# A linear-attention and mixture-of-experts kernel: tile loads widened to 128 rows, its start and early iterations reordered

## The chip, the cores and the metric

The kernel runs on one core of one Trainium2 chip, as one launch. The metric is device microseconds of that core, lower is better. The engines are TensorE (PE; its weight loads are shown as PEld), VectorE (DVE), ScalarE (ACT), GpSimd (POOL) and SyncE (SP), which issues most of the DMAs.

## The reference, cut to what matters

Three stages follow each other: a linear attention with a decay (4 batches, 8 heads, 768 positions, head size 48), an expert layer that sends each of the 3072 tokens to one of 8 experts, and a dense block with three gates. The change touches the first.

```python
for t in range(S):                       # 768 positions
    cur = einsum('bhd,bhe->bhde', u[None] * kt, vt)
    y[:, :, t] = einsum('bhd,bhde->bhe', rt, state + cur)
    state = wt[:, :, :, None] * state + einsum('bhd,bhe->bhde', kt, vt)
...
logits = x @ w_gate + modality_bias[modality_id]     # expert by argmax
out[mask] = gate_w[mask, None] * (max(x[mask] @ w1[e], 0) @ w2[e])
...
h = max(max(x @ w1, x @ w2), x @ w3);  return h @ w_out
```

Here rt, kt, vt and wt are the rows of r, k, v and w at position t.

## The kernel before, in words

The attention works on 24 tiles of 128 positions (6 per batch). A tile's r, k and w come transposed: 96 rows (a pair of heads of 48 channels each), and in the free dimension 3 x 4 head pairs x 128 positions. `load_t` brings them into one of four buffers `tq0` to `tq3`, in the 96 partitions from PAD = 16 on, so that each head lies in one half of the 128 partitions. The 16 partitions on both sides must hold harmless values: before the first tile, `pads` and some single fills write 0 for r and k and 1 for w to them (L768, L781 to L788, L798), and nothing overwrites them later. A second load, `load_n` (L816), brings the same tile with positions in partitions (`nat`: v, r and k).

For a tile, `flags` (L843, L845) checks the range of w with two ACT activations, `cut_w` (L854, L855) saves the last decay column of each head pair as `wl` and sets it to 0 in the buffer (times `keep`, which is 1 in the pad rows), so that one long scan over four head pairs starts afresh at each. `scan_f` (L861 to L865) takes the running product of the decays on DVE into the PSUM bank `prod`, `mul_r` (L870) multiplies r by it, `scan_r` (L875, L877) makes the reverse product, and `mul_k` (L882) multiplies k by that. PE then has `ktrans` (L904, copied by ACT as `kn`, L906), `scores` (L891, copied by ACT, L894, and masked by POOL, L895, as `am`), `kv` (L913, the tile's state contribution), `output` (L925, L931) and, behind DVE's `output_x` (L952, the output x), `columns` (L959, copied by ACT, L962) and `logits_of` (L239). `state_a` and `state_b` (L938, L943, L946) carry the state. The term with u goes over POOL (`uterm_a` L828 and L829, `uterm_b` L838) and a DVE sum (`usum` L834).

The order of the work is the order in which the code is written; every engine works its own instructions in that order and waits by semaphores. In iteration i of the main loop (L1017) DVE scans tile i + 2, PE transposes and scores tile i + 1 and makes the output of tile i; loads are issued some tiles ahead, and a load into a buffer waits until the tile that had it is done with it. `warm(n)` puts n filler matmuls on PE (L985); their numbers are in `WARM`. `rows()` (L174 to L221) prepares constants for the routing, in pieces that `slot()` puts into the iterations. From iteration 9 on, `route_between` routes tiles already done, and from iteration 13 on the first expert's weights are loaded. Behind the loop follow the last tiles, the rest of the routing, the experts and the dense block, which the change leaves as they are.

Of the kernel before, what the change touches and what calls it, by code (L numbers as in the profile page):

```python
# [23 lines left out]
P_LO = 1e-22  # L24
BIG = 1000000.0
# [18 lines left out]
WARM = (32, 20, 4, 0, 3, 0)  # L44
# [3 lines left out]
def kernel(ctx: ExitStack, tc: tile.TileContext, rkw_t, v_t, vrk, u, modality, w_gate, bias, w1, w2, v1, v2,  # L48
# [93 lines left out]
    flag = ct([128, NTILE, 2], F32, "flag")  # L142
# [587 lines left out]
    def attention(hooks):  # L730
        with ExitStack() as es:
# [35 lines left out]
            keep = e1.tile([128, 1], F32, name="keep")  # L767
            DVE.memset(tq[0][96:128, 1024:1536], 1.0)  # L768
            DVE.memset(wide, 0.0)
# [14 lines left out]
            def zeros(out, _):  # L784
                for q in range(2):
                    ACT.copy(out[:, q * 512:(q + 1) * 512], wide)
            POOL.memset(tq[0][96:128, 0:1024], 0.0)
            DVE.memset(tq[0][0:PAD, 1024:1536], 1.0)  # L788
            POOL.memset(neglo[:, 0:1], W_LO)
            POOL.memset(neglo[:, 1:2], -W_HI)  # L790
            POOL.memset(keep, 0.0)
            POOL.memset(keep[0:PAD], 1.0)
            POOL.memset(keep[96:128], 1.0)
            POOL.memset(keep[96:PAD + 2 * D], 0.0)
            DVE.memset(d1f, P_LO)
            DVE.memset(v4(d1f)[:, :, 0:1], 1.0)
            DVE.memset(d1r, 0.0)
            POOL.memset(tq[0][0:PAD, 0:1024], 0.0)  # L798
            pads(1, zeros)
            pads(2, DVE.memset, DVE.memset)  # L800
# [3 lines left out]
            pads(3)  # L804
# [35 lines left out]
            def flags(i):  # L840
                wr = tq[i % NB][:, 1024:1536]
                jk = a1.tile([128, 512], BF16, tag="jk", name="jk")
                ACT.activation(out=jk, in_=wr, func=ACTF.Relu, scale=-1.0, bias=neglo[:, 0:1],  # L843
                               accum_out=flag[:, i, 0:1])
                ACT.activation(out=jk, in_=wr, func=ACTF.Relu, scale=1.0, bias=neglo[:, 1:2],  # L845
                               accum_out=flag[:, i, 1:2])

            def cut_w(i):


                last = w_of(i)[:, :, 127:128]
                s = T[i]
                s["wl"] = a2.tile([128, HP, 1], F32, tag="wl", name="wl")
                ACT.copy(s["wl"], last)  # L854
                ACT.activation(out=last, in_=last, func=ACTF.Copy, scale=keep)  # L855

            def scan_f(i):

                s = T[i]
                f = tq[i % NB]  # L860
                DVE.tensor_tensor_scan(out=prod, data0=f[:, 1023:1535], data1=d1f, initial=0.0, op0=ALU.mult, op1=ALU.max)  # L861
# [3 lines left out]
                DVE.tensor_tensor(out=s["pt"], in0=end, in1=s["wl"], op=ALU.mult)  # L865
# [124 lines left out]
            load_t(0, [slice(q, q + 1) for q in (2, 0, 1)])  # L990
# [4 lines left out]
            load_n(1)  # L995
            loads()
            SP.dma_start(out=wg, in_=w_gate.rearrange("(k p) e -> p k e", p=128))
            load_n(2)
            warm(WARM[0])
            flags(0)  # L1000
            for i in range(2):
                cut_w(i)
                scan_f(i)
                mul_r(i)
                scan_r(i)
                mul_k(i)
                if i == 0:
                    flags(1)
                    ktrans(0)
                    scores(0)  # L1010
                    warm(WARM[1])
                uterm_a(i)
            load_t(3)
            load_t(4)
            flags(2)
            cut_w(2)
            for i in range(NTILE - 2):  # L1017
                n = i + 2
# [9 lines left out]
                if i:  # L1028
# [5 lines left out]
                uterm_a(n)  # L1034
# [13 lines left out]
                state_b(i)  # L1048
                slot()
                slot()  # L1050
                for j in (0, 1) if i == 0 else (i + 1,):
                    usum(j)
                    uterm_b(j)
# [10 lines left out]
                if i == 0:  # L1064
# [677 lines left out]
```

## Time and profile before

| | |
|---|---|
| median of 3 runs | 725.69 us (724.01 to 728.71) |
| profiled execution, its own time | 731.36 us |
| its span, from the first to the last instruction | 729.7 us |
| mean granted TensorE clock | 0.978 |
| busy share: PE, DVE, ACT, POOL | 96%, 63%, 45%, 45% |

The profile is of one execution; its span is what the timeline covers, and its own time has the launch around it. A busy engine is one that has an instruction under way; matmuls overlap, so a busy PE is not PE at its peak. Shares over the whole span are averages over stages with different limits.

### The profile page before, as it was taken

What the parts mean: (1) busy time and instruction counts of PE and PEld (TensorE: products, weight loads), DVE (VectorE), ACT (ScalarE), POOL (GpSimd) and SP (SyncE); (2) the same over time, 40 slices, a digit from 0 to 9 for tenths busy, and PEclk for the clock granted to TensorE, in tenths of its full rate; (3) what the DMA queues carried; (4) which work ended last, traced back from release to release, by engine and by line L of the source; (5) the groups of instructions that cost most, each with busy time, mean ns of one, the idle gap of its engine ahead of it and who ended that gap; (6) DMA issues with size and microseconds to landing.
All of it is one profiled execution on the core that took longest, in us unless ns stands there. A gap on an engine that the chain in (4) does not pass through costs nothing.

```text
span 729.7 us, 13002 instructions
## 1 busy us (share of the span) xinstructions
PE 697.3 (96%) x4891; PEld 629.5 (86%) x4892; DVE 456.2 (63%) x848; ACT 331.2 (45%) x720; POOL 326.1 (45%) x385
## 2 busy tenths in 40 slices
PE   8899999998799999999999999999999999999996
PEld 3788879787699999999999888988988989889886
DVE  6888988788395878998989758624234243142230
ACT  5576758764123576766667644321212212112111
POOL 5666667698736677768765424310200201101002
PEclk9899999999789999999999999999999999999998
DMA  8777769991023232232352633010200200000001
GB/s 248 219 225 214 232 171 208 251 284 47 12 67 90 86 109 66 87 87 67 121 196 66 226 108 108 19 69 0 82 6 0 88 1 11 33 1 33 11 1 48
DMA packets 29851, 72.98 MB, mean 100 GB/s; under 512 B 5109, under 2 KB 16149, under 8 KB 29780
## 3 DMA queue, kind: packets, MB, share of 16 engines
q1 hardware_dynamic: 25076, 62.58, 29.6%
q0 software_dynamic: 4704, 9.49, 4.1%
q8 instruction: 40, 0.66, 0.4%
q14 instruction: 31, 0.25, 0.1%
HBM read 83.04 MB, written 14.38 MB: 134 GB/s over the span
## 4 chain that ended last, share of the span: by engine, by line
issue 35%; PE 19%; POOL 5%; DVE 4%; ACT 2%; DMA 2%; POOLq 0%; DVEq 0%; ACTq 0%; SPq 0%
PE mm L1286 6%; PE mm L1287 6%; PE mm L1285 6%; POOL out_dram L1431 3%; DMA w2r<-in_moe_w_dram 2%; ACT w2h L636 1%; DVE w2l L638 1%; DVE t L689 1%; DVE hl L1299 1%; POOL vl L692 1%; DVE ya L678 1%; DVE ya L669 1%; PE tp L1274 0%; ACT hh L1298 0%; DVE ya L665 0%
## 5 line engine op out<-in xcount | busy, mean ns | idle before, releaser
L1411 DVE TENSOR_TENSOR w2r<-mm,w2r 128x512 f32<-128x512 f32 x72 | 49.7, 690 | 138.1 <-PE mm L1287 138.0
L1431 POOL DMA_INDIRECT out_dram<-w2r,oi_all x24 | 26.0, 1082 | 237.5 <-ACT w2r L1430 237.2
L1287 PE MATMUL mm<-w1h,vl 128*128 128x512 f32 x324 | 126.2, 389 | 0.0
L1286 PE MATMUL mm<-w1l,vh 128*128 128x512 f32 x324 | 126.2, 389 | 0.0
L1285 PE MATMUL mm<-w1h,vh 128*128 128x512 f32 x324 | 126.1, 389 | 0.0
L1286 PE MATMUL mm<-hl,w2h 128*128 128x256 f32 x288 | 83.1, 289 | 2.9 <-DVE hl L1299 2.8
L1285 PE MATMUL mm<-hh,w2h 128*128 128x256 f32 x288 | 83.8, 291 | 0.9 <-issue 0.9
L1287 PE MATMUL mm<-hh,w2l 128*128 128x256 f32 x288 | 82.5, 287 | 1.5 <-issue 1.5
L1413 ACT CAST w2h<-w2r 128x512 fp32r<-128x512 f32 x36 | 22.4, 621 | 129.6 <-DVE w2r L1411 129.6
L1285 PE MATMUL mm<-xh,w1h 128*128 128x256 f32 x282 | 81.0, 287 | 0.0
L1286 PE MATMUL mm<-xl,w1h 128*128 128x256 f32 x282 | 80.7, 286 | 0.3 <-issue 0.3
L1287 PE MATMUL mm<-xh,w1l 128*128 128x256 f32 x282 | 80.6, 286 | 0.0
L1287 PEld LDWEIGHTS mm<-w1h,vl 128*128 128x128 f32 x324 | 60.8, 188 | 12.7
L1286 PEld LDWEIGHTS mm<-w1l,vh 128*128 128x128 f32 x324 | 60.8, 188 | 12.5
L1285 PEld LDWEIGHTS mm<-w1h,vh 128*128 128x128 f32 x324 | 60.8, 188 | 12.4
L638 POOL TENSOR_TENSOR w2l<-w2r,w2h 128x384 fp32r<-128x384 f32 x44 | 50.1, 1143 | 33.1 <-ACT w2h L636 32.6
L1286 PEld LDWEIGHTS mm<-hl,w2h 128*128 128x128 f32 x288 | 56.4, 196 | 3.8 <-DVE hl L1299 3.8
L1285 PEld LDWEIGHTS mm<-hh,w2h 128*128 128x128 f32 x288 | 56.3, 196 | 2.9 <-issue 2.9
L1287 PEld LDWEIGHTS mm<-hh,w2l 128*128 128x128 f32 x288 | 56.3, 195 | 0.6 <-issue 0.6
L1286 PEld LDWEIGHTS mm<-xl,w1h 128*128 128x128 f32 x282 | 55.0, 195 | 0.5 <-issue 0.5
L1285 PEld LDWEIGHTS mm<-xh,w1h 128*128 128x128 f32 x282 | 55.0, 195 | 0.1
L1287 PEld LDWEIGHTS mm<-xh,w1l 128*128 128x128 f32 x282 | 54.9, 195 | 0.0
(338 smaller groups left out, 1647.1 us busy)
## 6 DMA issues: line engine op xcount, KB each, us to landing
w1r<-in_moe_w_dram SPq DMA_DIRECT2D x10, 1536.0 KB
w2r<-in_moe_w_dram SPq DMA_DIRECT2D x10, 1536.0 KB
nat<-in_vrk_dram SPq DMA_DIRECT2D x24, 608.0 KB
tq<-in_rkw_t_dram SPq DMA_DIRECT2D x23, 576.0 KB
stg<-in_moe_w_dram SPq DMA_DIRECT2D x18, 384.0 KB
x2t<-raw SPq DMA_DIRECT2D x12, 384.0 KB
w1r<-x2t SPq DMA_DIRECT2D x12, 384.0 KB
xs<-x SPq DMA_DIRECT2D x23, 192.0 KB
```

The costliest lines, as they stand in the source:

```text
L636: ACT.copy(hi, src)
L638: eng.tensor_tensor(out=lo, in0=src, in1=hi.bitcast(F32), op=ALU.subtract)
L669: DVE.tensor_scalar(out=yi, in0=yi, scalar1=3, scalar2=0x3FFFFFFF, op0=ALU.logical_shift_left, op1=ALU.bitwise_and)
L678: DVE.tensor_scalar(out=s["ya"].bitcast(I32), in0=s["t1"], scalar1=-0x800000, scalar2=None, op0=ALU.bitwise_and)
L689: DVE.tensor_tensor(out=tf, in0=tf, in1=hi.bitcast(F32), op=ALU.subtract)
L692: POOL.tensor_tensor(out=lo, in0=s["lf"], in1=s["t1"].bitcast(F32), op=ALU.add)
L1285: PE.matmul(oc, lhsT=wh[:, kk, sl], rhs=xh[:, kk, :], start=first and kk == 0, stop=False)
L1286: PE.matmul(oc, lhsT=wh[:, kk, sl], rhs=xl[:, kk, :], start=False, stop=False)
L1287: PE.matmul(oc, lhsT=wl[:, kk, sl], rhs=xh[:, kk, :], start=False, stop=last and kk == nk - 1)
L1411: DVE.tensor_tensor(out=hv, in0=o, in1=hv, op=ALU.max)
L1413: ACT.copy(self.h2h[:, c, :], hv)
L1431: ins = POOL.indirect_dma_start(out=out[:, :], out_offset=bass.IndirectOffsetOnAxis(ap=ids[q][:, 0:1], axis=0), in_=ob, in_offset=None, bo ...
```

## The change

A tile's load now covers all 128 partitions: since the 96-row blocks of all tiles follow each other in HBM, 16 rows of the block before and 16 of the block behind come along. For the first tile the rows before are missing (its load has 112 rows, and the fills for its first 16 partitions stay), for the last those behind (112 rows, and one fill of its last decay columns). No other buffer is filled beforehand. The foreign rows hold real numbers, so `mul_r` multiplies r also by `mine`, 1 in the tile's own 96 partitions and 0 elsewhere; the last column is set to 0 in all partitions; the product `pt` gets a lower bound, WL_LO. `flags` now comes after `cut_w`, and after `mul_k`, so it checks the 127 other columns; the last columns of all tiles are kept in `wlast` and checked once by `flags_last`. At the start r and k of tile 0 are loaded by ACT's queue and w by SP's, tile 1 is cut before the scores of tile 0, and loads, sums, outputs and filler matmuls of the first two iterations stand elsewhere; `rows()` begins after iteration 2 and no longer after iteration 0.

```diff
-WARM = (32, 20, 4, 0, 3, 0)
+WARM = (26, 9, 4, 0, 3, 0)
...
-            def pads(j, rk=POOL.memset, w=POOL.memset):
-                rk(tq[j][:, 0:1024], 0.0)
-                w(tq[j][:, 1024:1536], 1.0)
...
-            def load_t(i, parts=(slice(0, 3),)):
-                b, c = divmod(i, NC)
+            def load_t(i, parts=(slice(0, 3),), eng=SP):
+                lo = PAD if i == 0 else 0
+                hi = PAD + 2 * D if i == NTILE - 1 else 128
+                if i == NTILE - 1:
+                    POOL.memset(w_of(i)[:, :, 127:128], 1.0)
+                first = 2 * D * i - PAD
                 for q in parts:
-                    SP.dma_start(out=tq[i % NB][PAD:PAD + 2 * D, q.start * 512:q.stop * 512],
-                                 in_=rkw_t[b, c, :, :, q].rearrange("o d q a t -> (o d) (q a t)"))
+                    eng.dma_start(out=tq[i % NB][lo:hi, q.start * 512:q.stop * 512],
+                                  in_=all_t[first + lo:first + hi, q, :].rearrange("r q x -> r (q x)"))
...
-                ACT.activation(out=last, in_=last, func=ACTF.Copy, scale=keep)
+                ACT.activation(out=last, in_=last, func=ACTF.Copy, scale=0.0)
...
-                DVE.tensor_tensor(out=s["rt"], in0=r_of(i), in1=v4(prod), op=ALU.mult)
+                DVE.scalar_tensor_tensor(out=s["rt"], in0=r_of(i), scalar=mine, in1=v4(prod), op0=ALU.mult, op1=ALU.mult)
...
-            load_t(0, [slice(q, q + 1) for q in (2, 0, 1)])
+            load_t(0, [slice(0, 2)], ACT)
+            load_t(0, [slice(2, 3)])
             load_t(1)
             load_n(0)
             load_u()
             load_t(2)
             load_n(1)
+            load_t(3)
+            load_n(2)
             loads()
             SP.dma_start(out=wg, in_=w_gate.rearrange("(k p) e -> p k e", p=128))
-            load_n(2)
+            load_n(3)
             warm(WARM[0])
-            flags(0)
             for i in range(2):
                 cut_w(i)
                 scan_f(i)
+                flags(i)
                 mul_r(i)
                 scan_r(i)
                 mul_k(i)
-                if i == 0:
-                    flags(1)
-                    ktrans(0)
-                    scores(0)
-                    warm(WARM[1])
-                uterm_a(i)
-            load_t(3)
+            ktrans(0)
+            scores(0)
+            uterm_a(0)
+            warm(WARM[1])
+            cut_w(2)
             load_t(4)
-            flags(2)
-            cut_w(2)
             for i in range(NTILE - 2):
                 n = i + 2
-                if i + 5 < NTILE:
-                    load_t(i + 5)
                 kv(i)
...
+                if i == 1:
+                    output_x(0)
                 scan_f(n)
...
+                if i < 2:
+                    usum(i)
+                    uterm_b(i)
+                if i == 0:
+                    uterm_a(1)
+                if i == 1:
+                    warm(WARM[2])
...
-                if i + 3 < NTILE:
+                if 0 < i and i + 3 < NTILE:
                     load_n(i + 3)
+                if i + 5 < NTILE:
+                    load_t(i + 5)
                 output(i)
                 if i + 3 < NTILE:
-                    flags(i + 3)
                     cut_w(i + 3)
...
                 state_b(i)
+                flags(n)
+                if n == NTILE - 1:
+                    flags_last()
...
-                if i == 0:
+                if i == 2:
                     later.append(rows())
```

How this moves instructions on ACT at the start of the program, with the semaphores that each waits for (DMAHW are landings of loads), before; the tile buffers tq0 to tq3 are `tq_160` to `tq_163` here:

```order
L786 ACT_TABLE_LOAD
L786 CAST tq_161<-wide 128x512 [waits DVE_49]
L843 ACTIVATE jk,flag<-tq_160,neglo 128x512 [waits DMAHW0_49,DVE_49,Pool_49]
L845 ACTIVATE jk,flag<-tq_160,neglo 128x512 [waits Activation_49,Pool_49]
L854 COPY wl<-tq_160 128x4
L855 ACTIVATE tq_160<-tq_160,keep 128x4 [waits Activation_49,Pool_49]
L843 ACTIVATE jk,flag<-tq_161,neglo 128x512 [waits DMAHW3_49,Pool_49]
L845 ACTIVATE jk,flag<-tq_161,neglo 128x512 [waits Activation_49]
L906 COPY kn<-tp 128x512 [waits PE_49]
L894 COPY am<-mm 128x512 [waits PE_49] x2
L854 COPY wl<-tq_161 128x4
L855 ACTIVATE tq_161<-tq_161,keep 128x4 [waits Activation_49]
```

And now on the same engine and place; the buffers are `tq_161` to `tq_164`:

```order
L809 DMA tq_161<-in_rkw_t_dram 112x1024 [waits Pool_49]
L858 ACT_TABLE_LOAD [waits DMAHW0_49]
L858 COPY wlast<-tq_161 128x4 [waits DVE_49]
L859 ACTIVATE tq_161<-tq_161 128x4 [waits Activation_49]
L843 ACTIVATE jk,flag<-tq_161,neglo 128x4x127 [waits Pool_49]
L843 ACTIVATE jk,flag<-tq_161,neglo 128x4x127 [waits Activation_49,Pool_49]
L858 COPY wlast<-tq_162 128x4 [waits DMAHW1_49]
L859 ACTIVATE tq_162<-tq_162 128x4 [waits Activation_49]
L843 ACTIVATE jk,flag<-tq_162,neglo 128x4x127
L843 ACTIVATE jk,flag<-tq_162,neglo 128x4x127 [waits Activation_49]
L912 COPY kn<-tp 128x512 [waits PE_49]
L900 COPY am<-mm 128x512 [waits PE_49] x2
```

The cuts of tiles 0 and 1 (COPY wl or wlast and the ACTIVATE behind it) stand ahead of the checks and of tile 0's kn and am copies, and the table load stands behind the wait for the first decay load.

In a usual iteration, again on ACT, the rows before from the state copies of one iteration to those of the next:

```order
L946 COPY sbd_151<-stt_153 64x4x48 x2
L906 COPY kn<-tp 128x512
L894 COPY am<-mm 128x512 x2
L962 COPY xT<-tp 128x384
L843 ACTIVATE jk,flag<-tq_161,neglo 128x512
L845 ACTIVATE jk,flag<-tq_161,neglo 128x512
L854 COPY wl<-tq_161 128x4
L855 ACTIVATE tq_161<-tq_161,keep 128x4
```

And now:

```order
L952 COPY sbd_152<-stt_154 64x4x48 x2
L843 ACTIVATE jk,flag<-tq_162,neglo 128x4x127 x2
L912 COPY kn<-tp 128x512
L900 COPY am<-mm 128x512 x2
L968 COPY xT<-tp 128x384
L858 COPY wlast<-tq_164 128x4
L859 ACTIVATE tq_164<-tq_164 128x4
```

The cut follows the column copy xT directly; the two checks, of a tile whose k is already multiplied, stand between the state copies and the kn copy.

## Rows read from the trace of the kernel before

**Rows 1.** The page's busy time, share of the span and instructions of each engine.
```profile
PE 697.3 (96%) x4891; PEld 629.5 (86%) x4892; DVE 456.2 (63%) x848; ACT 331.2 (45%) x720; POOL 326.1 (45%) x385
```

**Rows 2.** Waits, 0 to 165 us: who waited for whom, us, times, longest.
```profile
DVE prod L861 <- ACT tq L855: 17.1, 14, 3.5
...
POOL nat L828 <- DMA nat<-in_vrk_dram: 7.1, 4, 4.1
DVE sh L834 <- POOL nat L829: 5.4, 5, 1.6
PE tp L959 <- DVE x L952: 5.2, 10, 1.6
```

**Rows 3.** Timeline, 0 to 41 us: start, duration, instruction [idle before <- ended by].
```profile
0.84 1.28 ACT L786 ACT_TABLE_LOAD   x1 [0.70 <-PEq L1727]
...
1.52 2.72 SPq L811 DMA_DIRECT2D tq<-in_rkw_t_dram  x4
...
4.27 0.72 ACT L843 ACTIVATE jk<-tq,neglo 128x512 bf16<-128x512 f32 x1 [1.00 <-DMA tq<-in_rkw_t_dram]
...
5.90 0.18 ACT L854 COPY wl<-tq 128x4 f32<-128x4 f32 x1
...
6.57 1.23 DVE L861 TENSOR_TENSOR_SCAN prod<-tq,d1f 128x512 f32<-128x512 f32 x1 [1.23 <-ACT tq L855]
...
8.72 0.72 ACT L843 ACTIVATE jk<-tq,neglo 128x512 bf16<-128x512 f32 x1 [2.24 <-DMA tq<-in_rkw_t_dram]
...
14.35 1.23 DVE L861 TENSOR_TENSOR_SCAN prod<-tq,d1f 128x512 f32<-128x512 f32 x1 [3.49 <-ACT tq L855]
...
18.73 1.23 DVE L861 TENSOR_TENSOR_SCAN prod<-tq,d1f 128x512 f32<-128x512 f32 x1
...
24.20 1.22 DVE L861 TENSOR_TENSOR_SCAN prod<-tq,d1f 128x512 f32<-128x512 f32 x1
...
25.60 0.89 DVE L178 CAST mf<-mi 24x128 f32<-24x128 int32 x1
...
32.00 0.36 DVE L191 CAST msk<-lgps 128x192 int32<-128x192 f32 x1 [2.36 <-PE lgps L187]
...
33.30 1.22 DVE L861 TENSOR_TENSOR_SCAN prod<-tq,d1f 128x512 f32<-128x512 f32 x1
...
40.72 1.23 DVE L861 TENSOR_TENSOR_SCAN prod<-tq,d1f 128x512 f32<-128x512 f32 x1 [1.96 <-ACT tq L855]
```

**Rows 4.** Timeline of PE and DVE over a usual iteration, 71 to 79 us.
```profile
71.76 0.67 PE L913 MATMUL lgps<-nat,kn 128*64 128x48 f32 x16
...
77.95 0.67 PE L913 MATMUL lgps<-nat,kn 128*64 128x48 f32 x16
...
78.51 1.23 DVE L861 TENSOR_TENSOR_SCAN prod<-tq,d1f 128x512 f32<-128x512 f32 x1 [0.91 <-ACT tq L855]
```

**Rows 5.** Windows: length; PE, PEld, DVE, ACT, POOL busy; clock, DMA share, GB/s.
```profile
16.00:22.00 6.00, 4.96 (x56) 3.80 (x55) 5.74 (x9) 2.28 (x5) 3.44 (x5) 1.00 1.02 274
22.00:29.00 7.00, 5.30 (x60) 4.18 (x59) 6.79 (x16) 4.86 (x13) 6.16 (x9) 1.00 0.89 248
29.00:36.00 7.00, 6.55 (x43) 5.81 (x44) 4.58 (x12) 2.03 (x9) 4.67 (x21) 0.51 0.55 173
...
130.00:155.00 25.00, 23.33 (x244) 20.13 (x245) 19.35 (x38) 16.24 (x43) 18.75 (x23) 1.00 1.03 257
155.00:160.00 5.00, 4.62 (x50) 3.93 (x47) 4.00 (x8) 4.06 (x11) 4.72 (x7) 1.00 1.01 367
```

**Rows 6.** Timeline: the multiplication of r, a scalar_tensor_tensor, the last score copies.
```profile
7.98 0.68 DVE L870 TENSOR_TENSOR rt<-tq,prod 128x512 f32<-128x512 f32 x1
...
168.74 1.07 ACT L894 COPY am<-mm 128x512 f32<-128x512 f32 x2 [2.06 <-PE mm L891]
...
185.32 0.69 DVE L1299 SCALAR_TENSOR_TENSOR hl<-d1r,hh 128x512 fp32r<-128x512 f32 x1 [2.07 <-ACT xe L962]
```

**Rows 7.** DMA view, 0 to 165 us: packets and bytes moved.
```profile
DMA packets 12312, 37.48 MB, mean 227 GB/s; under 512 B 2252, under 2 KB 6244, under 8 KB 12292
```

More of the change, by code (lines that the diff above doesn't have):

```diff
@@ L24 @@
 P_LO = 1e-22
+WL_LO = 1e-10
 BIG = 1000000.0
@@ L766, in attention @@
             tq = [e1.tile([128, 3 * 512], F32, name=f"tq{j}") for j in range(NB)]
-            keep = e1.tile([128, 1], F32, name="keep")
-            DVE.memset(tq[0][96:128, 1024:1536], 1.0)
-            DVE.memset(wide, 0.0)
+            mine = e1.tile([128, 1], F32, name="mine")
+            all_t = rkw_t.rearrange("b c o d q a t -> (b c o d) q (a t)")
+            POOL.memset(tq[0][96:128, 0:1024], 0.0)
             def r_of(i):
@@ L778, in w_of @@
                 return v4(tq[i % NB][:, 1024:1536])
-            def pads(j, rk=POOL.memset, w=POOL.memset):
-                rk(tq[j][:, 0:1024], 0.0)
-                w(tq[j][:, 1024:1536], 1.0)
[L784 to L787, printed above, removed]
-            DVE.memset(tq[0][0:PAD, 1024:1536], 1.0)
[L789 to L794, printed above, removed]
+            DVE.memset(wide, 0.0)
+            DVE.memset(tq[0][0:PAD, 1024:1536], 1.0)
             DVE.memset(d1f, P_LO)
@@ L797, in attention @@
             DVE.memset(d1r, 0.0)
+            DVE.memset(prod[:, 0:1], 1.0)
+            POOL.memset(neglo[:, 0:1], W_LO)
+            POOL.memset(neglo[:, 1:2], -W_HI)
+            POOL.memset(mine, 0.0)
+            POOL.memset(mine[0:64], 1.0)
+            POOL.memset(mine[64:96], 1.0)
+            POOL.memset(mine[96:PAD + 2 * D], 1.0)
+            POOL.memset(mine[0:PAD], 0.0)
             POOL.memset(tq[0][0:PAD, 0:1024], 0.0)
-            pads(1, zeros)
-            pads(2, DVE.memset, DVE.memset)
             make_identity(nc, ident)
@@ L840, in flags, with flags_last @@
             def flags(i):
-                wr = tq[i % NB][:, 1024:1536]
+                wr = w_of(i)[:, :, 0:127]
                 jk = a1.tile([128, 512], BF16, tag="jk", name="jk")
[L843 to L846, printed above, removed]
+                for q, sign in enumerate((-1.0, 1.0)):
+                    ACT.activation(out=v4(jk)[:, :, 0:127], in_=wr, func=ACTF.Relu, scale=sign, bias=neglo[:, q:q + 1],
+                                   accum_out=flag[:, i, q:q + 1])
+            def flags_last():
+                jk = a1.tile([128, 512], BF16, tag="jk", name="jk")[:, 0:NTILE * HP]
+                for q, sign in enumerate((-1.0, 1.0)):
+                    ACT.activation(out=jk, in_=wlast.rearrange("p t a -> p (t a)"), func=ACTF.Relu, scale=sign,
+                                   bias=neglo[:, q:q + 1], accum_out=flag[:, NTILE, q:q + 1])
             def cut_w(i):
@@ L860, in scan_f @@
                 f = tq[i % NB]
-                DVE.tensor_tensor_scan(out=prod, data0=f[:, 1023:1535], data1=d1f, initial=0.0, op0=ALU.mult, op1=ALU.max)
+                j = 1 if i == 0 else 0
+                DVE.tensor_tensor_scan(out=prod[:, j:512], data0=f[:, 1023 + j:1535], data1=d1f[:, j:512],
+                                       initial=float(j), op0=ALU.mult, op1=ALU.max)
                 end = v4(prod)[:, :, 127:128]
@@ L864, in scan_f @@
                 DVE.reciprocal(v4(d1r)[:, :, 126:127], end)
-                DVE.tensor_tensor(out=s["pt"], in0=end, in1=s["wl"], op=ALU.mult)
+                DVE.scalar_tensor_tensor(out=s["pt"], in0=s["wl"], scalar=WL_LO, in1=end, op0=ALU.max, op1=ALU.mult)
             def mul_r(i):
@@ L1048, in attention @@
                 state_b(i)
+                flags(n)
+                if n == NTILE - 1:
+                    flags_last()
                 slot()
                 slot()
-                for j in (0, 1) if i == 0 else (i + 1,):
-                    usum(j)
-                    uterm_b(j)
+                if i:
+                    usum(i + 1)
+                    uterm_b(i + 1)
+                if i == 0:
+                    uterm_a(n)
                 slot()
```

10 lines of the change are left out of this document (5 added, 5 removed).

## The prediction

> **What bounds the kernel now.** I read the page first: TensorE (PE) is busy for 96% of the span [rows 1]. So a gain in time must either take away idle or slow time of PE, or let it start sooner. After the attention stage (the first 165 us or so) PE runs the expert matmuls without such gaps, and the change does not touch them; all of the argument is on the attention stage, and a lead won there is carried to the end, because the stage behind it begins with the last tile's output.
>
> Next the waits of that stage [rows 2]. The one that the change aims at is VectorE's (DVE) forward scan at L861 waiting for ScalarE's (ACT) cut of the last decay column at L855: 17.1 us in 14 waits. But these waits are not all time lost, and the timeline shows where they are. At the start [rows 3]: the first scan begins at 6.57, after the first load was seen to land (4.27), two range checks on ACT (until 5.90) and the cut. The second begins at 14.35 after 3.49 idle, although tile 1 had landed by 8.72: ACT's cut of tile 1 stands behind the transposed copies and score copies of tile 0. Then the scans of tiles 2, 3, 4 and 5 begin at 18.73, 24.20, 33.30 and 40.72. In a usual iteration [rows 4] DVE again idles 0.91 us until the cut, but PE's rows for the same tile (71.76 to 77.95) are 6.19 us apart and PE is at work in between; DVE's idle time is hidden there. Only where PE itself waits for DVE is something lost: 5.2 us in 10 waits for the output x [rows 2].
>
> Last the windows [rows 5]: from 29 to 36 us the granted clock is 0.51, that is TensorE runs at 1.2 GHz and not 2.4, right after a stretch (22 to 29) in which PE was busy only 5.30 of 7.00 us. From 130 to 155 us the DMA share is 1.03 and GpSimd (POOL) is the late one: DVE waits 5.4 us for it and it waits 7.1 us for the nat loads [rows 2].
>
> **The change part by part.** Times are those of the profiled execution, 731.36 us; the median of the runs is 725.69, so I take the sum of differences from the one and subtract it from the other.
>
> Start. (a) The decay load of tile 0 waited for a fill of its upper rows and was issued at 1.52; 2.75 us later it had landed [rows 3]. The fill is gone, so it is issued at about 1.0 and lands at about 3.75. (b) Two checks stood between landing and cut, 4.27 to 5.90: 1.63 us, now behind the cut. From the cut's start to the scan it was 0.67. The two edits alone would give 0.52 + 1.63 = 2.15. (c) But the order of ACT's rows shows a new item on this path: ACT_TABLE_LOAD, 1.28 us [rows 3], ran at 0.84 under the first loads, since a copy of zeros came first on ACT. That copy is gone; the first activation is now the cut, and the table load stands behind its wait for the landing. So the scan begins at 3.75 + 1.28 + 0.67 = 5.7: 0.9 us earlier, not 2.15. I count 0.8.
>
> The r and k rows of tile 0 come on ACT's queue beside tile 1 on SP's. At the 274 GB/s of two queued tile loads [rows 5], 224 KB of w, 448 KB of r and k and as much of tile 1 take 4.2 us from about 3.0 on (the 2.75 us to landing less 0.7 for 192 KB, behind the issue at 1.0): 7.2. They are wanted when the scan and its small followers are done, at about 7.1. Cost 0, with 0.5 as the other end. The Trainium skill speaks against any bandwidth from the second queue (DMA: Bandwidth & Descriptors, section on issuing engines not being separate DMA queues: transfers from both engines interleave on the same 16 DMA engines, and only issue time is saved). By that rule, too, r and k share with tile 1 as reckoned here; no run here shows both queues yet.
>
> Tile 1. Its cut now precedes tile 0's score work, so the 3.49 us go, if tile 1 (1.44 MB queued in all, 5.4 us at the same rate, landed by about 8.4) is there before DVE is free at 10.1. Lead 4.3 us at tile 2 (14.4 for 18.73). The first iteration has one sum and one output on DVE where two sums stood: +0.1, tile 3 at 20.0. The second took 9.10 us (24.20 to 33.30): it held the routing constants (casts of 0.89 and 0.36, the second behind a wait of 2.36 for the transpose L187 [rows 3], and two copies of about that size: some 1.9 us and the wait) and the first half of the slow clock. Without those DVE's chain is about 6.1: lead 7.2 at tile 4. The third took 7.42, with 1.96 idle; as a usual one it takes 6.19: lead 8.4 at tile 5. PE then has matmuls, fillers included, for about all of each iteration, so I expect no fall of the clock. Fewer fillers (26 and 9 for 32 and 20) are no gain by themselves; they end before their followers are ready.
>
> Constants. They come three iterations later, where PE bounds. Their 1.9 + 2.4 us on DVE have some 0.9 of hidden idle in each of two iterations [rows 4] as cover, and the wait shrinks as DVE leads: cost 1.5, between 0 and 3.
>
> Usual iterations. The cut comes right after the column copy and no longer after 1.6 us of checks, so DVE starts up to 0.9 earlier; that is worth only PE's waits for x. Of their 5.2 us [rows 2] the longest (1.6) belongs to the start, counted already; of the other 3.6 I take 2.0, since some fall where POOL is late. The checks move behind the state copies and in front of the kn copy; ACT idles there for PE in every usual iteration, and PE's score copies follow it, so about 0.2 us of am could be late; PE takes am one iteration later, cost 0. On SP the tile load now follows nat and waits for the checks, two iterations before its use: cost 0. Multiplying r by mine as well makes L870 (0.68) a scalar_tensor_tensor, which at 128x512 took 0.69 elsewhere [rows 6]: 0.2 us over 24 tiles, on a hidden engine.
>
> Full-width loads. Bytes grow by 24 x 192 KB less two edges, 4.5 MB on 37.48 [rows 7]. From 130 to 155 the engines moved 257 GB/s at share 1.03, between 155 and 160 367 GB/s at 1.01 [rows 5]; the tile loads (two of them from 16 to 22) are the slow kind. If a load goes by its bytes, each takes a third longer; if by rows in the slowest of what they share, nothing. Bounds for the late stage: +6 (below) and -2 (nat earlier); I take 0, since PE there idles for POOL's own work more than for loads. The Trainium skill gives a reason for 0 (SBUF — State Buffer, section on the DMA port swizzle: partitions map to 16 ports by bits of their number). By its table, 96 rows from partition 16 put 8 rows on half of the ports and 4 on the others, and 128 rows put 8 on each, so the slowest port has the same load. By that rule late tile loads cost nothing, by bytes up to 6 us; the trace cannot tell yet.
>
> End. The checks of the last tile (1.6 as above) and of all last columns (by an estimate half of that) land on ACT ahead of the last score copies, which waited 2.06 [rows 6]: cost 0.3.
>
> Sum: 8.4 - 1.5 + 2.0 + 0 - 0.3 = 8.6. Forecast 725.7 - 8.6 = 717.1, say 717.
>
> **The rivals.**
> 1. The clock falls again in the first 35 us. For it: the start has about 1.5 us of PE idle between the shorter filler and tile 0's kt. Against: later iterations are full. At 0.51 the 7 us of that window lost 0.49 x 7 = 3.4 [rows 5], which would be given back: 720.5.
> 2. The lead shrinks in the POOL-bound stage: nat loads, behind fatter tile loads, land later. A third more on POOL's 7.1 us gives 2.4: 719.5.
> 3. On the other side: the DMA engines become the bound and a tile load goes by bytes. Place: the queue of the first loads, and 130 to 155 us. Four more loads with 0.79 MB on top of 6.4 MB need 289 GB/s there; below this they bind. At 257 GB/s eight late loads cost 1.57 MB / 257 = 6.1 us, and the five first ones 0.98 MB / 274 = 3.6: 717 + 9.7 = 726.7, slower than before.
> 4. More is won: the constants are hidden (1.5) and full-width loads, faster than 274 GB/s, halve POOL's waits for nat (about 2.5): 713.
> 5. The change does not do what it says: the table load takes all of the start's gain and the cut of tile 1 waits for its load. It would leave only the moved constants and the clock, about 4 us: 721.5.
>
> **How the numbers follow.** Forecast 0.50, rivals in their order 0.13, 0.12, 0.07, 0.13, 0.05. A measurement tells about 1% from no change, so faster means below 718.4: most of the forecast's own spread of some 2.5 us either way, all of rival 4, a third of rivals 1 and 2: 0.58. Slower means above 733, only the far end of rival 3: 0.03. Same: 0.39. The range leaves out the ends of rivals 3 and 4: 709 to 723.
>
> **What would show it.** Right: first scan at 5.7 with a table load in front of it, second scan without idle, scans of tiles 2 to 5 at about 14.4, 20.0, 26.1 and 32.3; granted clock 1.00 from 22 to 36; fewer waits of PE for x; the last tile's scan 8 to 9 us earlier; the expert part as long as before. Wrong: tile loads still queued when DVE wants a cut, a clock near 0.5 before 40 us, or a last scan less than 5 us earlier.

## The result and the profile after

The kernel after takes 729.96 us (median of 20 runs, 726.96 to 734.13), the kernel before, beside it, 726.01 us (20 runs, 723.66 to 731.14): a ratio of 1.0059, with an interval from 1.0041 to 1.0077. The forecast was 717 in a range of 709 to 723. The time went the other way by a little: 4 us slower, where 8.6 us less were expected.

The profile of after spans 727.7 us with a granted clock of 0.983. Against the profile of before, most of the lead in the attention stage is there, and it is lost later. The table has the start of the forward scan of each tile, in us, from the profiles (t23 is the last tile). The second profile of before and the run h_sp come from the experiments below; the forecast's figure for tile 1 is the moment at which it saw VectorE (DVE) free.

| scan of tile | before | before, second profile | forecast | after | h_sp |
|---|---|---|---|---|---|
| 0 | 6.57 | 6.42 | 5.7 | 5.49 | 5.30 |
| 1 | 14.35 | 14.51 | 10.1 | 12.58 | 9.74 |
| 2 | 18.73 | 18.89 | 14.4 | 17.02 | 14.18 |
| 3 | 24.20 | 24.35 | 20.0 | 23.46 | 19.58 |
| 4 | 33.30 | 32.35 | 26.1 | 28.88 | 25.01 |
| 5 | 40.72 | 38.21 | 32.3 | 34.66 | 31.39 |
| 6 | 46.87 | 44.90 | | 43.99 | 40.84 |
| 23 | 159.25 | 155.34 | | 151.60 | 151.23 |

The start of after, in its timeline (start, duration, instruction, idle before and what ended it), answers to [rows 3]:

```profile
0.83 0.88 SPq L809 DMA_DIRECT2D tq<-in_rkw_t_dram  x2
...
1.81 0.39 ACTq L809 DMA_DIRECT2D tq<-in_rkw_t_dram  x1
...
3.72 1.28 ACT L858 ACT_TABLE_LOAD   x1 [3.58 <-DMA tq<-in_rkw_t_dram]
...
5.49 1.23 DVE L866 TENSOR_TENSOR_SCAN prod<-tq,d1f 128x511 f32<-128x511 f32 x1 [2.45 <-ACT tq L859]
...
6.96 0.18 ACT L858 COPY wlast<-tq 128x4 f32<-128x4 f32 x1
...
9.54 0.75 DVE L876 SCALAR_TENSOR_TENSOR rt<-tq,mine,prod 128x512 f32<-128x512 f32 x1 [2.55 <-DMA tq<-in_rkw_t_dram]
...
12.58 1.23 DVE L866 TENSOR_TENSOR_SCAN prod<-tq,d1f 128x512 f32<-128x512 f32 x1
...
12.64 0.33 SPq L809 DMA_DIRECT2D tq<-in_rkw_t_dram  x1
12.64 0.66 PE L910 MATMUL tp<-ident,kt 128*128 128x128 f32 x3 [3.23 <-DVE kt L888]
```

The table load stands behind the landing, as forecast, and the first scan starts 0.2 us before its forecast. But r and k of tile 0, issued at 1.81 on ScalarE's (ACT) queue, come so late that DVE waits 2.55 us for them, until 9.54, while tile 1, from SyncE's (SP) queue, could be cut at 6.96. That issue waits for POOL (Pool_49 in the rows of the change), whose fill of partitions 96 to 127 of this buffer (L771) runs from 0.83 to 1.78; SP had issued w of tile 0 and tile 1 by 1.71. The fill is one more that the change keeps, though the load of 112 rows writes over all of it; a run without it was not made. TensorE (PE) then idles 3.23 us ahead of tile 0's transpose.

Later on the scans run on at a steady pace but for the iteration with the constants, between tiles 5 and 6 (DVE's timeline):

```profile
28.88 1.22 DVE L866 TENSOR_TENSOR_SCAN prod<-tq,d1f 128x512 f32<-128x512 f32 x1
34.66 1.23 DVE L866 TENSOR_TENSOR_SCAN prod<-tq,d1f 128x512 f32<-128x512 f32 x1 [0.26 <-ACT tq L859]
...
42.24 0.36 DVE L193 CAST msk<-lgps 128x192 int32<-128x192 f32 x1 [1.82 <-PE lgps L189]
...
43.99 1.21 DVE L866 TENSOR_TENSOR_SCAN prod<-tq,d1f 128x512 f32<-128x512 f32 x1
```

The waits from 0 to 165 us answer to [rows 2]: the wait for the cut falls from 17.1 to 7.9 us, that of PE for x from 5.2 in 10 to 1.7 in 2. Two rows of tile 0 are dearer: PE's wait for kt, 1.4 in two waits before, is 3.2 in one, and DVE's wait of 2.5 for the load of r is new.

```profile
DVE prod L866 <- ACT tq L859: 7.9, 9, 2.4
POOL nat L826 <- DMA nat<-in_vrk_dram: 5.9, 4, 3.0
...
DVE sh L832 <- POOL nat L827: 3.5, 5, 1.1
...
PE tp L910 <- DVE kt L888: 3.2, 1, 3.2
DVE rt L876 <- DMA tq<-in_rkw_t_dram: 2.5, 1, 2.5
...
PE tp L965 <- DVE x L958: 1.7, 2, 1.5
```

The windows answer to [rows 5] (busy PE, PEld, DVE, ACT, POOL; clock, DMA share, GB/s). The clock falls in the first of them, behind PE's idle 3.23 us, and no longer from 29 to 36. The loads run there at 402 GB/s (before: 320, in a line shown further down) at nearly the same DMA share:

```profile
10.00:17.00 7.00, 4.36 (x26) 2.93 (x27) 6.60 (x11) 1.96 (x5) 0.80 (x2) 0.76 1.02 402
29.00:36.00 7.00, 7.00 (x82) 6.44 (x83) 6.64 (x13) 5.57 (x15) 5.19 (x8) 1.00 0.55 163
...
130.00:155.00 25.00, 24.69 (x267) 21.44 (x267) 20.63 (x40) 16.68 (x44) 21.34 (x28) 1.00 0.93 306
```

At the last scan after is 7.65 us ahead of the profile of before. Most of that is lost in the stage that the change was not to touch. That stage is the dense block: its matmuls, with the weights vh and vl, begin at 427.29 us before and 418.14 after (the prediction and the expectations call them expert matmuls and expert weights). Its output rows, ACT's L1430 before and L1448 after (count, durations, first and last start), before:

```profile
L1430 ACT ACTIVATE w2r<-tp,oi_all x24: 570/582/586, 469.6 to 723.5; 128x384 f32<-128x384 f32 x24
```

and after:

```profile
L1448 ACT ACTIVATE w2r<-tp,oi_all x24: 570/582/584, 461.4 to 721.1; 128x384 f32<-128x384 f32 x24
```

The first of them is 8.2 us ahead, the last 2.4: 253.9 us have become 259.7. The groups of instructions on PE from 470 to 720 us (busy, mean ns) say where. Before:

```profile
L1287 PE MATMUL mm<-w1h,vl 128*128 128x512 f32 x270 | 105.1, 389 | 0.0
L1286 PE MATMUL mm<-w1l,vh 128*128 128x512 f32 x270 | 105.1, 389 | 0.0
L1285 PE MATMUL mm<-w1h,vh 128*128 128x512 f32 x270 | 105.0, 389 | 0.0
```

And after, in the same stretch:

```profile
L1303 PE MATMUL mm<-w1h,vh 128*128 128x512 f32 x269 | 106.6, 396 | 0.0
L1305 PE MATMUL mm<-w1h,vl 128*128 128x512 f32 x269 | 106.5, 396 | 0.0
L1304 PE MATMUL mm<-w1l,vh 128*128 128x512 f32 x269 | 105.7, 393 | 0.0
```

No idle time, the same instructions, each 4 to 7 ns longer. From start to start three of them take 680.7 ns before and 700.0 after (means of some 290 triples). There are 324 triples: 324 x 19.3 ns = 6.3 us.

The built programs say what differs there: the new constants (`wlast`, 384 bytes per partition, and a larger `flag`) stand ahead of everything that is allocated later, and so the dense block's weights vh, vl, voh and vol stand 416 bytes further: vh at byte 24448 of each partition where it stood at 24032. w1h and w1l, which hold the moving operand of these matmuls, lie in a pool at the other end and did not move (w1h: 157664).

### The profile page after: what moved, and what is told of

It is laid out like the page before. It is cut to its first block, busy times and chain, and to the rows that moved or that the text cites. A ratio compares the mean times of both kernels' runs of the same rounds, so it can differ in the third digit from the quotient of the medians.

```text
span 727.7 us, 12969 instructions
## 1 busy us (share of the span) xinstructions
PE 698.9 (96%) x4878; PEld 627.6 (86%) x4879; DVE 457.0 (63%) x846; ACT 329.5 (45%) x722; POOL 323.8 (45%) x384
## 3 DMA queue, kind: packets, MB, share of 16 engines
q1 hardware_dynamic: 25588, 66.64, 28.7%
## 4 chain that ended last, share of the span: by engine, by line
issue 37%; PE 32%; DVE 15%; POOL 7%; DMA 5%; ACT 3%; POOLq 0%; another core or an unknown queue 0%; DVEq 0%; SPq 0%; ACTq 0%
PE mm L1304 8%; PE mm L1303 7%; PE mm L1305 7%; DMA nat<-in_vrk_dram 4%; POOL out_dram L1449 3%; PE yb L931 2%; PE mm L897 1%; DVE prod L881 1%; PE lgps L241 1%; DMA tq<-in_rkw_t_dram 1%; DVE t L676 1%; DVE prod L866 1%; PE yb L937 1%; DVE hl L1317 1%; PE tp L1292 1%
## 5 line engine op out<-in xcount | busy, mean ns | idle before, releaser
L1305 PE MATMUL mm<-w1h,vl 128*128 128x512 f32 x324 | 128.4, 396 | 0.0
L1303 PE MATMUL mm<-w1h,vh 128*128 128x512 f32 x324 | 128.2, 396 | 0.0
```

The lines of the kernel that those rows point to most:

```text
L1303: PE.matmul(oc, lhsT=wh[:, kk, sl], rhs=xh[:, kk, :], start=first and kk == 0, stop=False)
L1305: PE.matmul(oc, lhsT=wl[:, kk, sl], rhs=xh[:, kk, :], start=False, stop=last and kk == nk - 1)
```

## The experiments

**Is it the place of the weights?** Four runs. In b_gap416 and a_gap32 a tile that nothing uses stands ahead of the weights:

```diff
         wres = pool(ctx, "wres", 1)
+        wres.tile([128, 104], F32, name="gap")
```

(8 columns instead of 104 in a_gap32). In a_home the constants that the change added leave the place that moves the weights:

```diff
-    wlast = ct([128, NTILE, HP], F32, "wlast")
...
-    slow = ct([128, 1], F32, "slow")
-    badw = ct([128, 1], F32, "badw")
+    slow_badw = ct([128, 2], F32, "slow_badw")
+    slow, badw = slow_badw[:, 0:1], slow_badw[:, 1:2]
...
             u_b = a1.tile([128, H, D], F32, name="u_b")
+            wlast = a1.tile([128, NTILE, HP], F32, name="wlast")
```

b_same is the kernel before, unchanged.

> The kernel before with 416 unused bytes per partition ahead of the expert weights vh, vl, voh, vol, so that these stand where the kernel after has them (24448 instead of 24032); nothing else differs. Theory 1, the place of the weights: from 465 us on three matmuls 128x512 (w1h,vh / w1l,vh / w1h,vl) take 700 ns from start to start as in the kernel after, not 680; 972 of them cost 6.5 us more, 0.9% slower (726.0 becomes 732.5). Theory 2, the new order of the attention leaves something behind that slows the expert part (transfers, code): three matmuls stay at 680 ns and the time within 0.2% of before.

> The kernel after with the tile of the last decay columns (wlast) in the attention's own pool and slow, badw in one tile, so that the expert weights start at 24032 again as in the kernel before; the order of instructions is that of after. Theory 1, the place of the weights: three matmuls take 680 ns, 730.0 becomes 723.5 (ratio to before 0.997 or lower). Theory 2, the order of the attention: they stay at 700 ns and the time at 730.

> The kernel after with 32 unused bytes ahead of the expert weights, which then start at 24480: the same place as before within 64 bytes (32), within 128 bytes (32 instead of 96) and within 512 bytes (416 instead of 480) another one. If only the place within 64 bytes counts, three matmuls take 680 ns and the span is 6.5 us shorter than that of after; if the place within 128 bytes or more counts, they take 700 ns or a third value; if the place is nothing (theory 2), 700 ns.

> The kernel before, unchanged, for a second profile and the granted clock of each of its runs. Theory A: the profile of before (span 729.7, clock 0.978, with TensorE at 1.2 GHz around 29-36 and 97-101 us) shows more falls of the clock than most of its runs have, whose median is 726.0: then this profile or most runs here have a clock of 0.985 or more, a span near 724, and of the 9.3 us by which the profile after was ahead at 400 us only some 5 are there in a usual pair of runs. Theory B: the falls are in every run, the clock is 0.978 in all of them, and the span of the profile is 729 to 730 again.

Measured: b_gap416 735.58 us for 729.25 of before on the same chip, ratio 1.0089 [1.0061, 1.0118]; three matmuls take 700 ns. a_home 725.27 us, ratio 0.9937 [0.9909, 0.9965]; three matmuls take 680. The kernel before, with an unused gap, is thus as slow in the dense block as after; and the change, without the move, is faster than before by 0.6%. Theory 1 holds, with the size of the forecast (6.5 us for b_gap416: 6.3). a_gap32 gave a third value, 687 ns, so the place within 64 bytes alone does not decide.

b_same, 0.9982 [0.9958, 1.0005], shows how the profile of before stands to other runs. From 29 to 36 us the second profile has its full clock:

```profile
29.00:36.00 7.00, 5.87 (x67) 5.27 (x67) 5.84 (x12) 4.22 (x12) 5.97 (x23) 1.00 0.68 222
```

The fall there in [rows 5] is an event of some executions: of the nine profiles in this study that have the attention of before (before, b_same, b_right160, b_both160 and the five b_gap runs), four have it, beginning between 28.7 and 29.5 us, and five do not. With it the scan of tile 5 comes at 40.7 to 42.1, without it at 38.2 to 38.7. At the scan of tile 6 the profile of before is 2.0 us behind b_same, at the last scan 159.25 - 155.34 = 3.9; the second half of this comes after tile 16 (113 us), where neither has a fall, and its cause is open. Theory A thus holds for the profiles: b_same spans 723.9 us with a clock of 0.985, and of the 9.2 us by which after leads the profile of before at the first matmul of the dense block, 3.3 are left against b_same (421.40). Theory B is wrong that every run has the falls. By the clock alone after's usual runs lose no less: its mean over the 20 runs of after is 0.982, over 23 runs of before on the chip of these four 0.982 too.

**What about the place decides?** The kernel before with gaps of 32, 64, 128 and 256 bytes, one run each:

> The kernel before with 32 unused bytes ahead of the expert weights (24064). Three matmuls 128x512 took 680 ns with the weights at 24032, 700 at 24448 (416 more) and 687 at 24480 (448 more). If the remainder by 64 bytes decides (32 before, 0 at 24448), 700 ns here. If the distance decides by some other measure, something between 680 and 700.

> 64 unused bytes (24096). The remainder by 64 bytes is that of before: 680 ns if it alone decides; as 448 more (the same remainder by 128 as here) gave 687, 687 if the remainder by 128 decides.

> 128 unused bytes (24160). 680 ns if the place within 128 bytes decides, another value if the place within 256 or 512 does.

> 256 unused bytes (24288). 680 ns if the place within 128 or 256 bytes decides, another value if the place within 512 does.

Then the other operand, moved alone (b_right160) and with the weights (b_both160), one run each:

```diff
             self.hl = p.tile([128, KF, TW], F32R, name="hl")
+            p.tile([128, 40], F32, name="gap2")
...
         wres = pool(ctx, "wres", 1)
+        wres.tile([128, 24], F32, name="gap")
```

> The kernel before with 160 unused bytes at the end of the pool of w1h, w1l, xh, xl, hh, hl: these move from remainder 224 by 256 bytes to 64, the expert weights stay at 24032 (remainder 224). In the matmuls of w1h,vh the weights vh then stand 160 bytes further within 256 than the moving w1h, as in the kernel after. If the distance between the two operands decides, three matmuls take 700 ns; if only the weights' own place decides, 680.

> b_right160 with 96 unused bytes ahead of the expert weights too (24128): both operands at remainder 64 by 256, neither where it was. If their distance decides, three matmuls take 680 ns again; if the weights' own place decides, 698 to 700, as with 64 and 128 unused bytes.

Measured, with the distance of the place of vh from that of w1h, both taken as remainders by 256:

| run | vh at | remainder of vh, w1h | distance | three matmuls |
|---|---|---|---|---|
| before, a_home | 24032 | 224, 224 | 0 | 680.8 ns |
| b_gap32 | 24064 | 0, 224 | 32 | 699.8 |
| b_gap64 | 24096 | 32, 224 | 64 | 699.9 |
| b_gap128 | 24160 | 96, 224 | 128 | 698.2 |
| after, b_gap416 | 24448 | 128, 224 | 160 | 700.0 |
| a_gap32 | 24480 | 160, 224 | 192 | 686.8 |
| b_gap256 | 24288 | 224, 224 | 0 | 680.8 |
| b_right160 | 24032 | 224, 64 | 160 | 700.0 |
| b_both160 | 24128 | 64, 64 | 0 | 680.7 |

The rules of 64 and of 128 bytes both fall with b_gap64 and b_gap128. At 256 bytes more the pace is that of before. b_right160 leaves the weights where they were and is slow; in b_both160 neither operand is where it was and it is fast. PE's groups from 470 to 690 us, of b_right160:

```profile
L1288 PE MATMUL mm<-w1h,vl 128*128 128x512 f32 x243 | 96.4, 397 | 0.0
L1286 PE MATMUL mm<-w1h,vh 128*128 128x512 f32 x243 | 96.0, 395 | 0.0
L1287 PE MATMUL mm<-w1l,vh 128*128 128x512 f32 x242 | 95.1, 393 | 0.0
```

and of b_both160:

```profile
L1287 PE MATMUL mm<-w1l,vh 128*128 128x512 f32 x251 | 97.7, 389 | 0.0
L1288 PE MATMUL mm<-w1h,vl 128*128 128x512 f32 x250 | 97.3, 389 | 0.0
L1286 PE MATMUL mm<-w1h,vh 128*128 128x512 f32 x250 | 97.2, 389 | 0.0
```

So the distance between the two operands decides, in the two pools that were tried, and of the distances tried 0 alone has full pace. The single times mostly go the same way: 732.64, 731.68, 730.04 and 725.74 us with gaps of 32, 64, 128 and 256 beside 729.23 of before; 727.89 for b_right160 and 717.35 for b_both160 beside 720.34.

This is the order for matmuls of 512 columns. The dense block's second product (128x384, moving voh and vol) is slowed by the same moves after another pattern: three of its matmuls take 521.2 ns at distance 0, 520.0 at 32 and 64, 527.9 at 128, 525.0 at 160 and 530.0 at 192. From before to after that is 144 x 3.8 ns = 0.5 us more.

**What is the rest of the change worth?** Four kernels on one chip (before: 721.29 us there), all made from a_home, so that the weights stand as before. h_old puts the calls back in the order of before and keeps the data path (loads of 128 rows, cut, `mine`, `wlast`):

```diff
-            load_t(0, [slice(0, 2)], ACT)
-            load_t(0, [slice(2, 3)])
+            load_t(0, [slice(q, q + 1) for q in (2, 0, 1)])
...
-            ktrans(0)
-            scores(0)
-            uterm_a(0)
-            warm(WARM[1])
-            cut_w(2)
+                if i == 0:
+                    flags(1)
+                    ktrans(0)
+                    scores(0)
+                    warm(WARM[1])
+                uterm_a(i)
+            load_t(3)
...
```

h_sp takes r and k of tile 0 to SP's queue, h_sp_tab loads the activation table early besides, h_rows0 puts the constants back:

```diff
-            load_t(0, [slice(0, 2)], ACT)
-            load_t(0, [slice(2, 3)])
+            load_t(0, [slice(2, 3), slice(0, 2)])
...
+            touch = e1.tile([128, 1], F32, name="touch")
+            ACT.copy(touch, wide[:, 0:1])
...
-                if i == 2:
+                if i == 0:
                     later.append(rows())
```

> a_home with its data path (foreign rows in the loads, no zeroing, scale 0 in the cut, wlast, mine) but the calls of the first tiles, of the loads and of the loop in the order of the kernel before (WARM 32, 20; rows() after the first iteration; flags ahead of the cut). Theory 1: the gain comes from the path, because the 3.49 us before the scan of tile 1 and the zeroing go: time within 1 us of a_home (725.3), 0.4 to 0.6% below before. Theory 2: it comes from the order (loads and flags moved, first tiles put in another order): time as before, 729, ratio 0.998 to 1.002, and the scan of tile 6 no earlier than 44.9 us, as in b_same.

> a_home with rows r, k of tile 0 loaded on SyncE's queue right behind w of tile 0 and ahead of tile 1, instead of on ScalarE's. Theory 1, the load on ScalarE's queue is served late beside those on SyncE's: mul_r(0) starts near 7.1 us instead of 9.5, the scan of tile 1 at 10.2 instead of 12.6, TensorE's idle time ahead of ktrans(0) falls from 3.2 to under 1 us, its clock does not fall at 11 to 18 us, and the time is 2.5 to 4 us below a_home (near 722). Rival, the DMA engines are simply full with 1.3 MB in those 9 us: tile 1 lands 2 us later instead, the scan of tile 1 waits for its cut, and the time is within 1 us of a_home.

> h_sp with a copy of one column on ScalarE that waits for the memset of wide alone (at 1.2 us), so that the activation table is loaded beside the first load and not behind its landing. Theory 1: the first scan starts at 4.2 us instead of 5.5 and all that follows up to the first matmul 1.0 to 1.3 us earlier; time 1 us below h_sp. Rival, r and k of tile 0 land at 7 us anyway: the first scan comes earlier and mul_r(0) waits for it, time as h_sp.

> a_home with the constants of rows() put back behind the first iteration instead of the third. Theory 1, their 1.5 to 2.5 us are paid wherever they stand among the iterations: the stretch of 9.3 us between the scans of tiles 5 and 6 falls to near 6.7, the scans of tiles 3 to 5 come that much later, the scan of tile 6 stands where it stood, time within 1 us of a_home. Rival: in the first iterations the engines wait for loads anyway and the constants cost nothing there: 2 us below a_home.

Measured:

| run | us | ratio to before |
|---|---|---|
| h_old | 719.50 | 0.9973 [0.9946, 1.0001] |
| a_home (other chip) | 725.27 | 0.9937 [0.9909, 0.9965] |
| h_rows0 | 716.86 | 0.9946 [0.9916, 0.9975] |
| h_sp | 713.97 | 0.9875 [0.9828, 0.9922] |
| h_sp_tab | 713.79 | 0.9888 [0.9847, 0.9930] |

h_old: its interval just reaches 1, so whether the data path alone gains anything cannot be told. The scan of tile 1 still comes at 14.73, the wait for the cut is longer than before (17.1) and PE's wait for x is as before (5.2):

```profile
DVE prod L866 <- ACT tq L859: 23.2, 19, 4.0
...
PE tp L965 <- DVE x L958: 5.0, 12, 1.6
```

The 3.49 us before that scan in [rows 3] therefore came from the order on ACT (cut of tile 1 behind tile 0's score copies), as the prediction said, and not from the zeroing: h_old has no zeroing, and that scan again idles 3.34 us for the cut, behind the copies of tile 0's scores. Theory 2 is the nearer one.

h_sp, in its timeline:

```profile
3.54 1.28 ACT L858 ACT_TABLE_LOAD   x1 [3.40 <-DMA tq<-in_rkw_t_dram]
...
5.30 1.23 DVE L866 TENSOR_TENSOR_SCAN prod<-tq,d1f 128x511 f32<-128x511 f32 x1 [2.26 <-ACT tq L859]
...
6.71 0.74 DVE L876 SCALAR_TENSOR_TENSOR rt<-tq,mine,prod 128x512 f32<-128x512 f32 x1
...
9.74 1.23 DVE L866 TENSOR_TENSOR_SCAN prod<-tq,d1f 128x512 f32<-128x512 f32 x1
9.79 0.63 PE L910 MATMUL tp<-ident,kt 128*128 128x128 f32 x4 [1.40 <-DVE kt L888]
```

The multiplication by r waits for nothing, the scan of tile 1 comes 2.84 us earlier than in after, PE's idle time is 1.40 and not 3.23 (theory 1 had put it under 1), and the clock holds. A window from 10 to 20 us, of a_home:

```profile
10.00:20.00 10.00, 6.92 (x45) 4.33 (x47) 9.00 (x16) 1.97 (x5) 3.19 (x4) 0.66 1.03 416
```

and of h_sp:

```profile
10.00:20.00 10.00, 9.41 (x102) 6.71 (x101) 9.60 (x18) 4.74 (x12) 6.48 (x9) 1.00 1.00 394
```

All four profiles with r and k on ACT's queue and the new order (after, a_home, a_gap32, h_rows0) have a fall of the clock that begins between 11 and 13 us; neither h_sp nor h_sp_tab has it. None of these six has the one at 29 us, and h_old, in the old order, has it. Theory 1 holds for the first tiles: the rival would have had tile 1 late, and it lands later (its cut waits for it until 7.91), but its scan does not wait. It is not shown that ScalarE's queue is the reason: h_sp changed the queue and the order of issue at once, and in after the load was issued behind tile 1. Nor do the profiles carry the 2.84 us to the end of the stage: h_sp and h_sp_tab have a fall beginning at 45.0 and 46.1 us, in the iteration with the constants (a_home has one at 49.3; after, a_gap32 and h_rows0 have none there), h_sp has another at 92.7, and its last scan is at 151.23, that of h_rows0, with r and k on ACT's queue, at 150.79.

h_sp_tab brings the first scan to 4.10, and it is given back within one tile:

```profile
4.10 1.23 DVE L868 TENSOR_TENSOR_SCAN prod<-tq,d1f 128x511 f32<-128x511 f32 x1 [1.06 <-ACT tq L861]
...
6.19 0.75 DVE L878 SCALAR_TENSOR_TENSOR rt<-tq,mine,prod 128x512 f32<-128x512 f32 x1 [0.58 <-DMA tq<-in_rkw_t_dram]
...
9.06 0.20 ACT L860 COPY wlast<-tq 128x4 f32<-128x4 f32 x1 [3.39 <-DMA tq<-in_rkw_t_dram]
...
9.54 1.23 DVE L868 TENSOR_TENSOR_SCAN prod<-tq,d1f 128x512 f32<-128x512 f32 x1 [0.39 <-DMA mi<-in_moe_modality_id_dram]
```

At tile 1 it is 0.2 us ahead of h_sp, at tile 2 it is not (14.54 for 14.18), and the times are the same: the rival, with the load of tile 1 after r and k as the next in line. Its cut waits for the landing until 9.06 (7.91 in h_sp), and the scan for the cut; that the last line names the small load mi, issued at 9.06, is a matter of how the profile finds what ended a wait.

h_rows0 has no long iteration before tile 6 (5.43 us and not 9.33),

```profile
39.41 1.22 DVE L866 TENSOR_TENSOR_SCAN prod<-tq,d1f 128x512 f32<-128x512 f32 x1
...
44.84 1.22 DVE L866 TENSOR_TENSOR_SCAN prod<-tq,d1f 128x512 f32<-128x512 f32 x1
```

but it is there at 44.84, a_home at 45.16; the ratio is a_home's. The constants are paid wherever they stand (theory 1).

## Why the prediction was wrong

**"The change does not touch them".** The step that failed first is in the first paragraph: the lead is carried to the end because the change does not touch the matmuls behind the attention stage. Their instructions it does not touch, but it moves operands of those in the dense block. The sum had no term for it. It cost 324 x 19.3 ns = 6.3 us, 0.9% as b_gap416 measured it alone. By b_gap416 and a_home together the change is 0.9937 x 1.0089 = 1.0025 (from 0.9969 to 1.0083 by the ends of the two intervals), which holds the 1.0059 that was measured. No rival had this; rival 3, the only one on the slower side, was another mechanism.

**"Cost 0, with 0.5 as the other end".** r and k of tile 0 on ACT's queue were to land at 7.2 and came 9.54 into the span. The trace's packets show why the sum was wrong: those of tile 1 ran from 2.70 to 5.41 us, the 4096-byte ones of ACT's queue only from 5.15 to 8.68, beside the nat load of SP's queue. The sum let r and k share the bandwidth from 3.0 us on with as much of tile 1; the runs showed them behind the whole of tile 1. Why is not settled. The load waited for the fill, which the sum does not have, and was issued at 1.81, behind both issues of SP, so its place in the order can be the reason as well as its queue; h_sp shows only that with r and k ahead of tile 1, on one queue, they are there at 6.71. The price is not the wait of 2.55 alone, since in all four profiles with r and k on ACT's queue and the new order a fall of the clock follows on PE's idle time ahead of kt (3.23 us in after, 4.00 to 4.52 in the others; 1.40 and 0.33 in h_sp and h_sp_tab, with none). Beside before, h_sp stands at 0.9875 and h_rows0, on the same chip, at 0.9946; the medians are 2.9 us apart and the intervals just touch, so some 3 to 5 us is an estimate, and the profiles do not show it at the last scan. The rule that was weighed there (the Trainium skill, DMA: Bandwidth & Descriptors, section on issuing engines not being separate DMA queues) speaks against a gain from the second queue. The trace agrees: the packets of r and k ran beside those of nat from SP's queue (4.79 to 8.67), and the DMA share was 1.01 from 4 to 8 us.

**"I expect no fall of the clock".** Rival 1, in the place named, behind PE's idle time between the filler and tile 0's kt, which became 3.23 and not 1.5 us. A clock of 0.76 over the 7 us from 10 to 17 is 1.7 us lost.

**"I take the sum of differences from the one and subtract it from the other."** Of the leads at tiles 4 and 5 a part was the slow clock from 29 to 36 us, which four of nine profiles of before's attention have. The new order does away with that fall, as forecast, but if four in nine is the usual share, the median of before holds it only in part: some 2.4 us at tile 5 (40.72 against 38.2 to 38.7) in about half of the executions. Against the second profile the lead of after at the last scan is 155.34 - 151.60 = 3.7 us, not the 8 to 9 forecast.

**"Cost 0.3" at the end.** A lead of DVE's scans is not yet one of PE. From the last scan to the first matmul of the experts the nine profiles with the attention of before take 16.3 to 16.8 us, but for two (before 18.1, b_gap32 17.6), the six with the new order 18.0 to 18.3. After, 3.7 us ahead of b_same at the last scan, is 2.1 ahead there (169.62 for 171.70); in the forecast this place had 0.3. The last checks do stand in front of ACT's last score copies; whether they take the 1.6 us was not tried.

**What held.** Start: 0.8 forecast, 6.42 - 5.49 = 0.9 against the second profile, with the table load where it was seen. The chain of the first tiles: with r and k in time, h_sp's scans of tiles 1 to 5 lie within 1.1 us of the forecast. Usual iterations: 2.0 forecast; from the scan of tile 6 to the last take 108.9 us in b_gap416 (45.39 to 154.32) and 105.9 in h_rows0 (44.84 to 150.79), neither with a fall of the clock between: 3.0, with all that the wider loads do in the late stage in it. Constants: the extra of the long iteration is 9.33 - 5.43 = 3.9 us, above the 0 to 3 forecast, but the lead at tile 4 had been credited with it; moved, they cost and give nothing. Full-width loads: 0 forecast, and no cost by bytes shows. From 10 to 17 us before moved

```profile
10.00:17.00 7.00, 6.60 (x43) 3.36 (x41) 3.41 (x7) 4.35 (x13) 3.52 (x5) 1.00 1.05 320
```

320 GB/s at a share of 1.05, after 402 at 1.02; from 130 to 155 us 257 GB/s at 1.03 [rows 5] became 306 at 0.93, and POOL's wait for nat fell from 7.1 to 5.9 us. Rivals 2 and 3 are out. The rule for 0 (the Trainium skill, SBUF — State Buffer, section on the DMA port swizzle) agrees with these numbers; that the ports are the reason was not tried apart.

The forecast's 8.6 us are 1.2%; h_sp, the change without its two faults, is 1.25% faster than before (0.8 to 1.7). That the two numbers meet is in part luck, since the lead that they were to come from was counted too high. Of the 12.9 us between 717.1 and 730.0 the operands' distance is 6.3, shown alone; the order of the first loads with the fall behind it is an estimated 3 to 5; the rest, the fall counted in full and the end, is not parted run by run.

## What to carry to other kernels

An edit that allocates a few hundred bytes moves everything that is allocated behind it. Compare the places of the operands of the costliest matmuls before and after such an edit, and look at the mean ns of groups that were "not touched" first: 389 against 393 to 396 ns, in 972 matmuls, was enough to turn 0.6% faster (a_home) into 0.6% slower. A lead of one engine at the end of its stage is worth what the engine behind it starts earlier. Issue the loads at the start in the order in which they are wanted, and look at what each issue itself waits for; here the load that was wanted first was issued behind another. And look whether a slow stretch of the clock is in more than one profile of the kernel before, before all of it is counted as something to win.

## What was not expected of the hardware

Matmuls of 128x512 float32r with 128x128 weights, back to back, follow each other after 227 ns when weights and moving operand start at the same remainder by 256 bytes per partition, and after 229 (distance 192) to 233 ns (distances 32 to 160) when not. All are means of a triple (680.7 to 700.0 ns) at the full clock, in eleven kernels with these five other distances and 0. The weight load itself takes 188 ns in either case; only the pace of the pair differs. The Trainium skill (SBUF — State Buffer, section on the two separate sides) says that on the engines' side only the port pair shared by VectorE and GpSimd causes contention; the rows here show up to 3% that hang on where TensorE's own two operands stand to each other, and where the page and the rows differ the rows decide. That the two reads meet is the nearest reading and was not tried apart. With 384 columns the pattern is another (520 ns for three at distances 32 and 64, 530 at 192), so the rule of distance 0 holds for 512 columns alone; why, and whether other types have it, is open.
